# A fused attention and mixer kernel on one core: half of the second row's probabilities turned by DMA, its values in two float16 parts

## The chip, the core and the metric

The kernel runs on one core of one Trainium2 chip. The metric is device time in microseconds (us) of one execution. The engines are TensorE (PE, with its weight loads as PEld), VectorE (DVE), ScalarE (ACT), GpSimd (POOL) and SyncE (SP, which here issues nearly all DMA transfers).

## The reference

Two batch rows of 768 positions go through three stages. q and k are scaled random normals, v is 0.1 times a random normal; n_global is 8 and n_local 96, so each query tile of 128 positions sees its own tile, the one before it, and a few global columns.

```python
scores = scale * q @ k.T - slope[h] * dist        # 8 heads of 64; masked where not keep
a = exp(scores - max); a = a / (sum(a) + 1e-9)
x = (a @ v)                                        # 2 x 768 x 512
x = x + relu(layernorm(x) * g @ w_ch1) @ w_ch2     # 512 -> 2048 -> 512
u = x + (relu(x.T @ w_tok1) @ w_tok2).T            # over the 768 positions, 256 wide
out = u + relu(u @ w_ch1') @ w_ch2'                # 512 -> 1536 -> 512
```

## The kernel before

The work is cut into 12 row tiles T of 128 positions: T = 0 to 5 are the first batch row, T = 6 to 11 (`SPLIT` = 6 and up) the second. All float32 products of the MLPs are made of three float16 products: each factor is split into a high and a low part, and `mm3` (L372 to L374) adds high x high, high x low and low x high in PSUM.

Attention of one tile is `window_tile` (L400). It handles the 8 heads in four pairs p. For each two pairs PE makes the scores (L453, a PSUM tile `S`); DVE adds bias and takes the row minimum (L469, tile `ex`); ACT takes the exponential (L474); PE turns the probabilities, 128x128 at a time, by float32 transposes against an identity (L479, PSUM tile `T`). From there the rows differ:

- First row: ACT or DVE copies the turned probabilities to `pt` (L515, L518), and PE multiplies by V in float32 (L484).
- Second row: ACT writes their float16 high part `ph`, scaled by 2^15 (L501), DVE the rest `pl` (L503), and `pv3` multiplies on PE by V, which is held in three bfloat16 parts `vb` with a column of ones: three matmuls per head and key block, of 130, 64 and 130 columns (L497 to L499). The three parts of V cost two casts and two subtractions per tile (L423 to L430: one cast on DVE, one on ACT, both subtractions on GpSimd). A pair has four transposes and 12 such matmuls; in tile 6, which has one key block only, half of that.

In all 24 pairs of the second row there are 88 transposes and 88 groups of three matmuls.

Then come layer norm (`norm_ops`), a float16 split of the normed tile and its transposition by a DMA on SP (`turn_ops`, L580, tiles `xh` to `xa` or `xb`), and the first MLP in passes over groups of three tiles. Attention is spread between the MLP's matmuls. Weights come as doubles: SP loads 512 KB to `stg` (L166), ACT and DVE repack them (L744 `fw`, L750 `wf`) and split them (L766, L772 or L769 on GpSimd); the split weights are stored to DRAM (L725) and loaded again for later passes (L715).

The order of every engine's instructions is made ahead of time by a planner (`Plan`). Each operation has an engine, an estimated cost and a due time `prio`; the constants `AHEAD`, `SLOT`, `DUE`, `EARLY`, `LEAD`, `HEAD` and others set the due times, and strings such as `LOB1` or `FE` say which engine takes which operation. While PE would have nothing to do in the first stretch, the planner puts in filler matmuls (L106). Each engine then runs its own queue strictly in this order; SP's queue too, so a transfer that waits holds back the ones behind it.

`Guard` collects sums of squares of inputs and intermediate tiles (ACT, L671) and checks at the end that all lie in ranges in which the float16 splits are exact enough; if not, a slow general path runs again.

Of the kernel before, what the change touches and what calls it, by code (L numbers as in the profile page):

```python
# [12 lines left out]
F16 = mybir.dt.float16  # L13
# [17 lines left out]
PSC = 2.0 ** 15  # L31
# [361 lines left out]
def copy_on(nc, eng, out, src):  # L393
    if eng == "A":
        nc.scalar.activation(out=out, in_=src, func=AF.Copy)
    else:
        nc.vector.tensor_copy(out, src)


def window_tile(o, plan, prio, T, slot):  # L400
# [41 lines left out]
    for p in range(4):  # L442
# [89 lines left out]
        if p == 3 and 0 < t < NT - 1:  # L532
# [100 lines left out]
class Guard:  # L633
# [4 lines left out]
          "z": (86, 90, 0.0, 60000.0), "g": (90, 91, 0.125, 16.0)}  # L638
    N = 91
# [430 lines left out]
AHEAD = {'s': -8.81, 'k': 53.46, 'q': -8.16, 'v': 42.47}  # L1070
STORE, RELOAD = 53.17, 7.48

LOA1 = 'GVGGVVVVVGGVVGVV'
LOB1 = 'GGGGVGVGVGVVGVVV'
LOA2 = 'GGGVVVVVVGVG'
LOB2 = 'VVVVVVGVVVGV'
LOT = 'VGG'
NLO, ULO = 'GGVGGGGGVVGV', 'VGVVVGVGGVVG'
TURN = 2.5
UP = 19.85  # L1080
MK0, MK1, MK2 = 'VVVVAAAA', 'VAVVAAAA', 'AVVVAVAA'
# [19 lines left out]
WIDE = {'hid': 5, 'wa': 5, 'wb': 5, 'stg': 3, 'fw': 2, 'wf': 2, 'st': 2, 'xn': 1, 'mn': 3, 'sum': 3, 'ex': 3, 'pt': 2, 'ph': 2, 'pl': 2, 'ao': 2, 'xz': 3, 'sx': 8, 'raw0': 1, 'raw1': 1, 'xa': 1, 'xb': 1, 'm': 2, 'k': 2, 's': 2, 't': 2}  # L1101
SIZES = {**WIDE, 'hid': 12, 'wa': 8, 'wb': 8, 'wf': 4, 'fw': 3, 'stg': 4, 'xn': 2, 'xh': 2, 'uh': 2, 'xz': 3, 'sz': 4}

# [178 lines left out]
class WindowAttention:  # L1282
    def __init__(self, o):
# [5 lines left out]
        o.vb = ap.tile([P, 3, H, 3, D + 1], BF16, name="vb")  # L1289

    def ops(self, o, plan, prio):
# [3 lines left out]
        plan.op("G", 0.3, 20.0, lambda: nc.gpsimd.memset(o.vb[:, :, :, 0, D:], 1.0), w=[("vb", z, 0) for z in range(3)])  # L1295
        plan.op("G", 0.5, 20.0, lambda: nc.gpsimd.memset(o.vb[:, :, :, 1:, D:], 0.0), w=[("vb", z, i) for z in range(3) for i in (1, 2)])
# [179 lines left out]
```

## Time and profile before

| what | us |
|---|---|
| median of 3 runs | 553.74 (553.57 to 555.43) |
| the profiled execution | 554.65 |
| its span, first to last instruction | 552.9 |
| PE busy | 543.2 |
| DVE busy | 408.9 |
| ACT busy | 334.9 |
| POOL busy | 178.0 |

The mean granted clock of PE is 0.993 of full speed. The span is read from the profile's page; the 1.75 us between it and the execution's time lie around it. A matmul's duration in the trace covers its way through the array, and consecutive matmuls overlap; what a matmul costs the queue is the distance from its start to the next one's start. In the same way ACT and DVE instructions overlap their neighbours by some 0.1 us, so their cost is read as start to start.

### The profile page before, as it was taken

The numbers are of one execution on the slowest core, as the hardware profiler recorded it, in microseconds if no ns is written. First come the engines' busy times: TensorE is split into PE (matmuls) and PEld (weight loads), VectorE is DVE, ScalarE is ACT, GpSimd is POOL, SyncE is SP. The second block draws the span as 40 slices with busy tenths as digits, with TensorE's granted clock in tenths as the row PEclk, the third lists the DMA queues.
The fourth block names the chain that finished last, engine by engine and source line by source line (L and its number), as shares of the span: only waits on it lengthen the run. The fifth ranks groups of instructions, "written<-read, shape, count | busy, mean of one in ns | idle before, by whom it ended". The sixth has DMA issues, their size and how long they took to land.

```text
span 552.9 us, 9384 instructions
## 1 busy us (share of the span) xinstructions
PE 543.2 (98%) x3267; PEld 310.7 (56%) x3267; DVE 408.9 (74%) x909; ACT 334.9 (61%) x747; POOL 178.0 (32%) x185
## 2 busy tenths in 40 slices
PE   8999999999999999999999999999999999999995
PEld 6777766746656555554555555455445545555542
DVE  7778889977599554579888986899987777654431
ACT  6778778966848334745877655667785554534210
POOL 2233574660411023363322236502151563110000
PEclk9999999999999999999999999999999999999998
DMA  8877997796869757312674460047564342302012
GB/s 252 217 194 230 236 279 238 202 287 203 272 238 282 258 106 185 111 58 61 187 178 157 162 152 21 1 153 223 201 181 123 107 157 77 115 1 76 2 39 82
DMA packets 87596, 87.09 MB, mean 158 GB/s; under 512 B 46836, under 2 KB 61172, under 8 KB 87540
## 3 DMA queue, kind: packets, MB, share of 16 engines
q1 hardware_dynamic: 87538, 86.40, 53.6%
q8 instruction: 28, 0.46, 0.4%
q14 instruction: 28, 0.23, 0.1%
q10 hardware_dynamic: 2, 0.00, 0.0%
HBM read 61.87 MB, written 17.83 MB: 144 GB/s over the span
## 4 chain that ended last, share of the span: by engine, by line
PE 94%; DVE 2%; ACT 2%; issue 1%; POOL 0%; POOLq 0%; ACTq 0%
PE L L372 12%; PE L L374 12%; PE L L373 12%; PE L2S L374 9%; PE L2S L373 9%; PE L2S L372 9%; PE chain L372 4%; PE chain L374 4%; PE chain L373 4%; PE S L453 4%; PE T L479 3%; PE PV L484 2%; PE tok L374 2%; PE tok L372 2%; PE tok L373 2%
## 5 line engine op out<-in xcount | busy, mean ns | idle before, releaser
L372 PE MATMUL L2S<-wb,h 128*128 128x512 f16 x228 | 86.4, 379 | 0.0
L373 PE MATMUL L2S<-wb,h 128*128 128x512 f16 x228 | 86.4, 379 | 0.0
L374 PE MATMUL L2S<-wb,h 128*128 128x512 f16 x228 | 86.4, 379 | 0.0
L889 DVE SCALAR_TENSOR_TENSOR x<-L2S,x 128x512 f32<-128x512 f32 x57 | 39.2, 688 | 49.7 <-PE L2S L374 49.7
L374 PEld LDWEIGHTS <-h 128*128 128x128 f16 x336 | 32.9, 98 | 39.6
L744 ACT ACTIVATE fw<-stg 128x512 f16<-128x512 bf16 x62 | 48.0, 776 | 10.5 <-DMA stg<-in_moe_w_ch_dram 7.2
L372 PEld LDWEIGHTS <-h 128*128 128x128 f16 x336 | 32.8, 98 | 36.8 <-issue 0.7
L373 PEld LDWEIGHTS <-h 128*128 128x128 f16 x336 | 32.9, 98 | 35.8
L474 ACT ACTIVATE ex<-ex,mn 128x256 f32<-128x256 f32 (+1 forms) x96 | 41.6, 480 | 14.1 <-DVE mn L469 13.9
L823 POOL TENSOR_TENSOR sz<-Q,sz 128x512 f16<-128x512 f32 x18 | 22.4, 1242 | 84.6 <-ACT sz L915 84.6
L750 DVE SCALAR_TENSOR_TENSOR wf<-stg,fw 128x512 uint32<-128x512 uint32 x62 | 44.8, 736 | 0.4 <-DMA scr_1b<-wb 0.4
L372 PE MATMUL L<-wb,h 128*128 128x512 f16 x108 | 41.0, 379 | 0.0
L374 PE MATMUL L<-wb,h 128*128 128x512 f16 x108 | 40.9, 379 | 0.0
L373 PE MATMUL L<-wb,h 128*128 128x512 f16 x108 | 40.9, 379 | 0.0
L364 DVE SCALAR_TENSOR_TENSOR h<-L,h 128x384 f16<-128x384 f32 x40 | 22.2, 555 | 22.5 <-ACT h L358 22.2
L823 POOL TENSOR_TENSOR Q<-wa 128x512 f32<-128x512 f16 x18 | 25.9, 1438 | 38.8 <-DVE wa L772 18.5
L372 PEld LDWEIGHTS <-wa 128*128 128x128 f16 x268 | 26.2, 98 | 19.6 <-issue 2.7
L374 PEld LDWEIGHTS <-wa 128*128 128x128 f16 x268 | 26.2, 98 | 17.3
L373 PEld LDWEIGHTS <-wa 128*128 128x128 f16 x268 | 26.2, 98 | 17.0
L889 DVE SCALAR_TENSOR_TENSOR x<-L,x 128x512 f32<-128x512 f32 x27 | 18.6, 690 | 22.2 <-PE L L374 22.1
L372 PE MATMUL L<-xa,wa 128*128 128x384 f16 x104 | 34.0, 326 | 0.0
L373 PE MATMUL L<-xa,wa 128*128 128x384 f16 x104 | 33.9, 326 | 0.0
(233 smaller groups left out, 1417.7 us busy)
## 6 DMA issues: line engine op xcount, KB each, us to landing
stg<-in_moe_w_ch_dram SPq DMA_DIRECT2D x56, 512.0 KB, 4.6
wa<-scr_1a SPq DMA_DIRECT2D x24, 256.0 KB, 3.7
wb<-scr_1b SPq DMA_DIRECT2D x24, 256.0 KB, 4.0
scr_1a<-wa SPq DMA_DIRECT2D x16, 256.0 KB, 6.8
scr_1b<-wb SPq DMA_DIRECT2D x16, 256.0 KB, 3.5
K<-in_k_dram SPq DMA_DIRECT2D x12, 256.0 KB, 3.9
Q<-in_q_dram SPq DMA_DIRECT2D x12, 256.0 KB, 4.4
V<-in_v_dram SPq DMA_DIRECT2D x12, 256.0 KB, 4.0
```

What stands on the lines that cost most here:

```text
L364: nc.vector.scalar_tensor_tensor(out=lo(), in0=src(), scalar=0.0, in1=plain(hi()), op0=ALU.max, op1=ALU.subtract)
L372: nc.tensor.matmul(ps, ah, bh, start=first, stop=False, **k)
L373: nc.tensor.matmul(ps, ah, bl, start=False, stop=False, **k)
L374: nc.tensor.matmul(ps, al, bh, start=False, stop=last, **k)
L453: nc.tensor.matmul(bs[j].t[:, i, :w], o.Q[r, qs, p + i, :], o.K[r, slots, p + i, :], start=True, stop=True)
L474: nc.scalar.activation(out=ex.t[:, j, :w], in_=ex.t[:, j, :w], func=AF.Exp, bias=mn.t[:, h:h + 1], scale=-1.0)
L479: nc.tensor.transpose(bt.t[:, j, i, :], ex.t[:, j, i * P:(i + 1) * P], o.ident[:])
L484: nc.tensor.matmul(bv.t[:, 2 * (p % 2) + j], pt.t[:, j, i, :], o.V[:, z, 2 * p + j], start=(i == 0), stop=(i == n - 1))
L744: op("A", 0.66, prio - 2, lambda: nc.scalar.activation(out=fw.t[:, :, 1], in_=stg.t[:, 4:2049:4].bitcast(BF16), func=AF.Copy, scale=2.0 if ...
L750: op("V", 0.6, prio - 1, lambda: nc.vector.scalar_tensor_tensor(out=raw().bitcast(U32), in0=stg.t.bitcast(U32)[:, 1:1024:2], scalar=13, in ...
L823: op(eng, {"G": 0.1 + n * 0.00227, "V": 0.07 + n * 0.00104}[eng], prio, lambda: e.tensor_tensor(out=out(), in0=a(), in1=b(), op=alu), lock ...
L889: n = op("V", 0.6, prio, lambda: nc.vector.scalar_tensor_tensor(out=x[:], in0=b.t[:], scalar=BACK if o.half else 1.0, in1=x[:], op0=ALU.mu ...
```

## The change

1. V of the second row is held in two float16 parts, scaled by 2^8, not three bfloat16 parts. Per tile ACT writes the high part (`AF.Copy` with scale), DVE the low part (`scalar_tensor_tensor`), and ACT a sum of squares of V for the range check (kind "v", six more columns). GpSimd's two subtractions and one cast go away.
2. `pv3` issues two matmuls per head and key block, of 130 columns (high probabilities x both parts of V) and of 65 (low probabilities x high part of V), not three.
3. A string `PT` marks each of the 24 pairs of the second row P or D; 12 are D: two of tile 6, two of tile 8, one of tile 9, four of tile 10, three of tile 11. For a D pair ("turned") ACT and DVE split the unturned probabilities `ex` into a tile `pq` of 8 blocks, and one DMA transpose on SP's queue turns all of them into `ph`. The PE transposes and their PSUM tile go away for it. The D pairs of tile 6 have 4 blocks, the ten others 8. So 10 x 4 + 2 x 2 = 44 PE transposes are gone.
4. The planner's constants and engine strings are set anew, which orders everything anew.

```diff
-        op("G", 1.15, pvr, lambda: nc.gpsimd.tensor_tensor(out=v, in0=v, in1=V[:, :, 0, :D], op=ALU.subtract),
-           r=[("vb", c, 0)], w=[("v", c)])
...
-        op("G", 1.15, pvr, lambda: nc.gpsimd.tensor_tensor(out=V[:, :, 2, :D], in0=v, in1=V[:, :, 1, :D], op=ALU.subtract),
-           r=[("v", c), ("vb", c, 1)], w=[("vb", c, 2)])
+        op("A", 0.54, pvr, lambda: nc.scalar.activation(out=V[:, :, 0, :D], in_=v, func=AF.Copy, scale=VSC), r=[("v", c)],
+           w=[("vb", c, 0)])
+        op("V", 0.6, pvr, lambda: nc.vector.scalar_tensor_tensor(
+            out=V[:, :, 1, :D], in0=v, scalar=VSC, in1=V[:, :, 0, :D], op0=ALU.mult, op1=ALU.subtract),
+           r=[("v", c), ("vb", c, 0)], w=[("vb", c, 1)], lock=True)
+        o.guard.square("v", pvr + GUARDX, lambda: v, [("v", c)])
...
-                        nc.tensor.matmul(bv.t[:, j], ph.t[:, j, i, :], o.vb[:, z, h, 0:2], start=(i == 0), stop=False)
-                        nc.tensor.matmul(bv.t[:, j, 1, :D], ph.t[:, j, i, :], o.vb[:, z, h, 2, :D], start=False, stop=False)
-                        nc.tensor.matmul(bv.t[:, j], pl.t[:, j, i, :], o.vb[:, z, h, 0:2], start=False, stop=(i == n - 1))
...
+                        a = j * n + i
+                        nc.tensor.matmul(bv.t[:, j], pt.t[:, a], o.vb[:, z, h], start=(i == 0), stop=False)
+                        nc.tensor.matmul(bv.t[:, j, 0], pt.t[:, 2 * n + a], o.vb[:, z, h, 0], start=False, stop=(i == n - 1))
...
+            op("A", 0.06 + 0.23 * n if turned else 0.05 + 0.215 * n, prio(k + slot["T"]), lambda part=part, src=src: nc.scalar.activation(
+                out=part(0), in_=src(), func=AF.Copy, scale=PSC), r=keys, w=dst[:1], get=[pq] if turned else [])
+            op("V", 0.3 * n, prio(k + slot["T"]), lambda part=part, src=src: nc.vector.scalar_tensor_tensor(
+                out=part(1), in0=src(), scalar=PSC, in1=part(0), op0=ALU.mult, op1=ALU.subtract),
+               r=[*keys, dst[0]], w=dst[1:], lock=turned)
+            if turned:
+                op("S", TURN * n / 2, prio(k + slot["T"]), lambda pt=pt, pq=pq: nc.sync.dma_start(
+                    pt.t[:, :4 * n], pq.t[:, :4 * w], transpose=True), r=dst, w=[(pt, 0), (pt, 1)], get=[pt])
...
-AHEAD = {'s': -8.81, 'k': 53.46, 'q': -8.16, 'v': 42.47}
+AHEAD = {'s': 29.29, 'k': 79.79, 'q': -33.06, 'v': -59.46}
...
+PT = 'PDPDPPPPDPDPPPPDDDDDDDDP'
...
-HEAD = 85.06
-DUE = [36.2, 20.0, 77.7, 9.05]
+HEAD = 56.45
+DUE = [32.72, 16.66, 78.81, 48.03]
```

What this moves is shown at three places.

**TensorE, attention of tile 10, before.** An MLP matmul, then the transposes of two pairs (`T`), then the next MLP matmuls; 24 rows further on the first group of three value matmuls (`PV`).

```order
L374 LDWEIGHTS wa_1968
L374 MATMUL L1_2462<-xb_897,wa_1968 128x384
L479 MATMUL T_2488<-ident_127,ex_2450 128x128 x4
L479 MATMUL T_2495<-ident_127,ex_2454 128x128 x4
L372 LDWEIGHTS wa_1976
```

```order
L497 LDWEIGHTS ph_2489
L497 MATMUL PV_2530<-vb_232,ph_2489 128x130
L498 LDWEIGHTS ph_2489
L498 MATMUL PV_2530<-vb_232,ph_2489 128x64
L499 LDWEIGHTS pl_2490
L499 MATMUL PV_2530<-vb_232,pl_2490 128x130
```

**The same stretch of TensorE after** (a turned pair of tile 10).

```order
L373 MATMUL L1_2294<-xb_914,wa_1909 128x384
L374 LDWEIGHTS wa_1909
L374 MATMUL L1_2294<-xb_914,wa_1909 128x384
L498 LDWEIGHTS ph_2256
L498 MATMUL PV_2323<-vb_232,ph_2256 128x130
L499 LDWEIGHTS ph_2256
L499 MATMUL PV_2323<-vb_232,ph_2256 128x65
```

The transposes of a turned pair are gone from this queue, and a group is two matmuls; the 65-column one reads the blocks of the low part from the same tile `ph`.

**SP's queue in the same stretch, before**: weight loads (`stg`), stores and reloads of split weights (`scr`, `wb`), a load of global K columns and a copy inside `vb`.

```order
L535 DMA K_58<-in_k_dram 128x4x32
L160 DMA K_58<-in_k_dram 128x512
L715 DMA wb_2059<-scr_1b4_1978 128x1024
L715 DMA wb_2064<-scr_1b5_2002 128x1024
L715 DMA wb_2099<-scr_1b6_2015 128x1024
L725 DMA scr_1b7_2116<-wb_1571 128x1024
L166 DMA stg_61<-in_moe_w_ch1_dram 128x4x512
L539 DMA vb_232<-vb_232 32x1560
L166 DMA stg_61<-in_moe_w_ch1_dram 128x4x512
L715 DMA wb_2175<-scr_1b7_2116 128x1024
L166 DMA stg_61<-in_moe_w_ch1_dram 128x4x512
L166 DMA stg0_203<-in_moe_w_ch1_dram 128x4x512
```

**After:**

```order
L515 DMA_TRANSPOSE ph_2033<-pq_1990 128x8x128
L166 DMA stg_61<-in_moe_w_ch2_dram 128x2048 x2
L515 DMA_TRANSPOSE ph_2110<-pq_2066 128x8x128
L550 DMA vb_232<-vb_232 32x1040
L546 DMA K_58<-in_k_dram 128x4x32
L515 DMA_TRANSPOSE ph_2144<-pq_2083 128x8x128
L166 DMA stg_61<-in_moe_w_ch2_dram 128x2048
L515 DMA_TRANSPOSE ph_2188<-pq_2148 128x8x128
L166 DMA stg0_203<-in_moe_w_ch2_dram 128x2048
L166 DMA stg_61<-in_moe_w_ch1_dram 128x4x512
L515 DMA_TRANSPOSE ph_2256<-pq_2190 128x8x128
L166 DMA stg_61<-in_moe_w_ch1_dram 128x4x512
```

The DMA transposes of turned pairs stand between the weight loads; each waits for DVE's second part of `pq`, and the `stg` loads behind it are issued after it. The reloads of this pass stand ahead of the stretch.

**ScalarE in the head, before**: from the first exponentials of tile 3 to the split of the normed tile 2 (`xh`). `fw` and `wa` or `wb` are weights being repacked and split.

```order
L474 ACTIVATE ex_612<-ex_612,mn_613 128x256 x2
L744 ACTIVATE fw1_63<-stg_61 128x512
L474 ACTIVATE ex_628<-ex_628,mn_613 128x256
L515 ACTIVATE pt_634<-T_633 128x512
L474 ACTIVATE ex_628<-ex_628,mn_613 128x256
L744 ACTIVATE fw2_204<-stg_61 128x512
L766 ACTIVATE wa_667<-wf_651 128x512
L515 ACTIVATE pt_661<-T_660 128x512
L613 ACTIVATE xn_679<-x2_66,st_654 128x512
L474 ACTIVATE ex_669<-ex_669,mn_613 128x256 x2
L474 ACTIVATE ex_674<-ex_674,mn_613 128x256 x2
L576 ACTIVATE xh_700<-xn_679 128x512
```

**After**, up to the norm of tile 2 (`xn`):

```order
L755 ACTIVATE fw2_204<-stg_61 128x512
L777 ACTIVATE wa_638<-wf_619 128x512
L526 ACTIVATE pt_624<-T_623 128x512
L473 ACTIVATE ex_630<-ex_630,mn_631 128x256 x2
L473 ACTIVATE ex_642<-ex_642,mn_631 128x256 x2
L755 ACTIVATE fw0_62<-stg_61 128x512
L526 ACTIVATE pt_658<-T_657 128x512
L777 ACTIVATE wa_686<-wf_655 128x512
L526 ACTIVATE pt_681<-T_680 128x512
L777 ACTIVATE wb_694<-wf_677 128x512
L755 ACTIVATE fw1_63<-stg0_203 128x512
L624 ACTIVATE xn_711<-x2_66,st_689 128x512
```

More weight work stands between the exponentials: until the 40th exponential (the end of tile 4) ScalarE's queue now holds 11 `fw` where it held 6, 8 splits of weights where it held 4, and 16 copies `pt` where it held 14.

## Rows read from the trace of the kernel before

**Rows 1.** The page's part 1: busy us, share of the span, instructions of each engine.

```profile
PE 543.2 (98%) x3267; PEld 310.7 (56%) x3267; DVE 408.9 (74%) x909; ACT 334.9 (61%) x747; POOL 178.0 (32%) x185
```

**Rows 2.** Windows: stretch, length, PE, PEld, DVE, ACT, POOL busy; PEclk, DMA share, GB/s.

```profile
0.00:20.00 20.00, 18.04 (x122) 13.46 (x122) 15.66 (x74) 14.28 (x40) 4.28 (x32) 1.00 0.89 254
20.00:40.00 20.00, 19.40 (x155) 16.11 (x155) 15.42 (x61) 14.41 (x31) 7.16 (x11) 1.00 0.69 180
40.00:58.00 18.00, 17.08 (x117) 13.19 (x116) 13.31 (x47) 16.48 (x35) 5.71 (x7) 0.91 0.78 232
58.00:80.00 22.00, 22.00 (x173) 15.65 (x172) 18.15 (x60) 15.60 (x36) 14.47 (x13) 1.00 1.00 259
80.00:110.00 30.00, 30.00 (x257) 20.62 (x254) 27.56 (x72) 27.54 (x64) 16.94 (x15) 1.00 0.77 225
110.00:150.00 40.00, 40.00 (x276) 23.34 (x274) 26.94 (x64) 28.56 (x67) 14.70 (x14) 1.00 0.80 249
150.00:200.00 50.00, 50.00 (x355) 29.98 (x354) 38.03 (x92) 28.02 (x54) 5.86 (x6) 1.00 0.72 236
200.00:552.00 352.00, 346.70 (x1830) 178.31 (x1828) 253.80 (x445) 190.02 (x428) 108.90 (x92) 1.00 0.40 114
```

**Rows 3.** Waits of PE: line, what it waited for, us in total, times, longest.

```profile
PE T L479 <- ACT ex L474: 0.8, 2, 0.4
PE PV L484 <- ACT pt L515: 0.6, 1, 0.6
```

**Rows 4.** Chain that ended last, three pieces: start us, us, what.

```profile
31.37 1.06 PE S L453 x8
...
40.58 2.01 PE S L453 x8
...
152.07 0.44 PE T L479 x4
```

**Rows 5.** Timeline of PE at two pairs of the second row: start, duration, instruction.

```profile
196.62 0.33 PE L374 MATMUL L<-xa,wa 128*128 128x384 f16 x1
196.79 0.22 PE L497 MATMUL PV<-vb,ph 128*128 128x130 bf16 x1
196.84 0.20 PE L498 MATMUL PV<-vb,ph 128*128 128x64 bf16 x1
196.88 0.22 PE L499 MATMUL PV<-vb,pl 128*128 128x130 bf16 x1
196.93 0.22 PE L497 MATMUL PV<-vb,ph 128*128 128x130 bf16 x1
...
197.96 0.33 PE L372 MATMUL L<-xb,wa 128*128 128x384 f16 x1
```

**Rows 6.** Line L580, the DMA transposes: issue time ns and landing us, min/median/max.

```profile
L580 SPq DMA_TRANSPOSE xb<-xh x9: 1232/1238/1289, 54.4 to 428.4; - x9
...
DMA to landing us min/median/max: 3.0/3.2/6.2
```

**Rows 7.** Groups of ACT and of DVE: count, busy us, mean ns, idle before.

```profile
L501 ACT ACTIVATE ph<-T 128x512 f16<-128x512 f32 (+1 forms) x24 | 12.5, 559 | 6.3 <-PE T L479 6.2
L671 ACT ACTIVATE junk<-x 128x512 bf16<-128x512 f32 x24 | 14.9, 622 | 16.0 <-DVE x L889 15.2 <-DVE x L1057 0.6
L503 DVE SCALAR_TENSOR_TENSOR pl<-T,ph 128x512 f16<-128x512 f32 (+1 forms) x24 | 14.6, 640 | 1.4 <-ACT ph L501 1.3
```

**Rows 8.** Timeline of ACT in the head: start, duration, instruction.

```profile
45.14 0.62 ACT L766 ACTIVATE wa<-wf 128x512 f16<-128x512 f32 x1
45.66 0.89 ACT L474 ACTIVATE ex<-ex,mn 128x256 f32<-128x256 f32 x2
46.46 0.77 ACT L744 ACTIVATE fw<-stg 128x512 f16<-128x512 bf16 x1
47.10 0.56 ACT L515 ACTIVATE pt<-T 128x512 f32<-128x512 f32 x1
47.56 0.50 ACT L474 ACTIVATE ex<-ex,mn 128x256 f32<-128x256 f32 x1
```

More of the change, by code (lines that the diff above doesn't have):

```diff
@@ L460, in window_tile @@
         pt = Buf("pt", lambda: o.sm.tile([P, 2, 2, P], F32, tag="pt", name="pt", bufs=2))
-        bt = psum_buf(o, "T", [2, 2, P])
+        turned = T >= SPLIT and PT[4 * (T - SPLIT) + p] == "D"
+        bt = None if turned else psum_buf(o, "T", [2, 2, P])
         if T >= SPLIT:
-            pt = Buf("ph", lambda: o.sm.tile([P, 2, 2, P], F16, tag="ph", name="ph", bufs=2))
-            pl = Buf("pl", lambda: o.sm.tile([P, 2, 2, P], F16, tag="pl", name="pl", bufs=2))
+            pt = Buf("ph", lambda: o.sm.tile([P, 8, P], F16, tag="ph", name="ph", bufs=o.sizes["ph"]))
+            pq = Buf("pq", lambda: o.sm.tile([P, 8 * P], F16, tag="pq", name="pq", bufs=o.sizes["pq"]))
             bv = psum_buf(o, "PV", [2, 2, D + 1])
@@ L490, in window_tile, with pv3 @@
             op("A", 0.3 if n == 1 else 0.4, prio(k + slot["exp"]), lambda j=j, expo=expo: expo(j), r=[(mn, p, j)], w=[(ex, j)])
-        op("T", 0.22 * n, prio(k + slot["T"]), probs, r=[(ex, 0), (ex, 1)], w=[(bt, 0)], get=[bt, pt] + ([pl] if T >= SPLIT else []))
+        if not turned:
+            op("T", 0.22 * n, prio(k + slot["T"]), probs, r=[(ex, 0), (ex, 1)], w=[(bt, 0)], get=[bt, pt])
         if T >= SPLIT:
-            def pv3(p=p, ph=pt, pl=pl, bv=bv):
+            def pv3(p=p, pt=pt, bv=bv):
                 for j in range(2):
@@ new lines, in pv3 @@
+                        nc.tensor.matmul(bv.t[:, j, 0], pt.t[:, 2 * n + a], o.vb[:, z, h, 0], start=False, stop=(i == n - 1))
+            if turned:
+                part = lambda i, y=pq: y.t[:, i * 2 * w:(i + 1) * 2 * w].rearrange("p (j c) -> p j c", j=2)
+                src = lambda ex=ex: ex.t[:, :, :w]
+                keys, dst = [(ex, 0), (ex, 1)], [(pq, 0), (pq, 1)]
+            else:
+                part = lambda i, y=pt: y.t[:, i * 2 * n:(i + 1) * 2 * n].rearrange("p (j i) c -> p j i c", j=2)
+                src = lambda bt=bt: bt.t[:, :, :n]
+                keys, dst = [(bt, 0)], [(pt, 0), (pt, 1)]
@@ L507, in window_tile @@
+            if turned:
+                op("S", TURN * n / 2, prio(k + slot["T"]), lambda pt=pt, pq=pq: nc.sync.dma_start(
+                    pt.t[:, :4 * n], pq.t[:, :4 * w], transpose=True), r=dst, w=[(pt, 0), (pt, 1)], get=[pt])
+            op("T", 0.18 * n, prio(k + slot["PV"]), pv3, r=[(pt, 0), (pt, 1), *vkeys], w=[(bv, 0)], get=[bv])
             if PVE[T - SPLIT] == "A":
@@ L539, in window_tile @@
                 op("S", 0.3, prio(k + slot["gk"]), lambda: nc.sync.dma_start(o.vb[:NGF, c], o.vb[:NGF, prev]),
-                   r=[("vb", prev, i) for i in range(3)], w=[("vb", c, i) for i in range(3)])
+                   r=[("vb", prev, i) for i in range(2)], w=[("vb", c, i) for i in range(2)])
     if T >= SPLIT:
         def inverse():
-            nc.vector.tensor_scalar(out=sm.t[:], in0=ao.t[:, :, 0, D], scalar1=1e-9 * PSC, scalar2=None, op0=ALU.add)
+            nc.vector.tensor_scalar(out=sm.t[:], in0=ao.t[:, :, 0, D], scalar1=1e-9 * PSC * VSC, scalar2=None, op0=ALU.add)
             nc.vector.reciprocal(out=sm.t[:], in_=sm.t[:])
@@ L1065, in token_ops @@
         transpose_ops(o, plan, prio(14 + 2 * i), "uT", lambda T=T: o.x[T][:], [*xk(T), ("tk",), *r], dst, key, get)
-AHEAD = {'s': -8.81, 'k': 53.46, 'q': -8.16, 'v': 42.47}
[L1071 to L1081, printed above, removed]
+AHEAD = {'s': 29.29, 'k': 79.79, 'q': -33.06, 'v': -59.46}
+STORE, RELOAD = 42.03, 10.48
+LOA1 = 'VGGVVGGVGVGGVVGG'
+LOB1 = 'GGVGVVGGGVVGGGGV'
+LOA2 = 'VGVVVGVVVGGG'
+LOB2 = 'VVGVGGVGVVGG'
+LOT = 'GGG'
+NLO, ULO = 'VGVVVVVVVGGG', 'GGGGVGVGGGVV'
+TURN = 2.2
+PT = 'PDPDPPPPDPDPPPPDDDDDDDDP'
+UP = -65.03
+MK0, MK1, MK2 = 'VVVVAAAA', 'AAVAAAAV', 'AAVAVVAV'
 HEAD0 = -200.0
-MASK2 = -121.51
+MASK2 = -122.88
 BUSY = 10, 3
-HOLD = [-39.73, 27.18, 27.27]
+HOLD = [-99.44, -5.02, 7.93]
 FIRST = [("k", 0), ("q", 0), ("k", 1), ("q", 1), ("v", 0), (1, "a", 0), ("v", 1), (1, "a", 1), ("k", 2), ("q", 2), (1, "a", 2), ("v", 2)]
@@ L1100 @@
 PSUMS = ('m', 's', 't', 'k')
[L1101 to L1102 removed]
+WIDE = {'hid': 5, 'wa': 5, 'wb': 5, 'stg': 3, 'fw': 2, 'wf': 2, 'st': 2, 'xn': 1, 'mn': 3, 'sum': 3, 'ex': 3, 'pt': 2, 'ph': 2, 'pq': 2, 'ao': 2, 'xz': 3, 'sx': 8, 'raw0': 1, 'raw1': 1, 'xa': 1, 'xb': 1, 'm': 2, 'k': 2, 's': 2, 't': 2}
+SIZES = {**WIDE, 'hid': 12, 'wa': 8, 'wb': 8, 'wf': 4, 'fw': 3, 'stg': 4, 'xn': 2, 'ph': 3, 'pq': 2, 'xh': 2, 'uh': 2, 'xz': 3, 'sz': 4}
 def store(o, T):
@@ L1288, in __init__ @@
         o.bmh = ap.tile([P, H, 3, P], BF16, name="bmh")
-        o.vb = ap.tile([P, 3, H, 3, D + 1], BF16, name="vb")
+        o.vb = ap.tile([P, 3, H, 2, D + 1], F16, name="vb")
     def ops(self, o, plan, prio):
```

44 lines of the change are left out of this document (17 added, 27 removed).

## The prediction

> **What bounds the kernel now.** I read the busy times first, then PE by stretch, then PE's waits, the chain of work that ended last, and at last the places that the edit touches. PE is busy for 543.2 of 552.9 us [rows 1]. By stretch [rows 2] it has no gap at all from 58 to 200 us, where attention of the second row runs between the MLP's matmuls, and what it lacks after 200 us is the tail behind its last matmul. Before 58 us it is short of work: 2.0, 0.6 and 0.9 us of gaps in three windows, filler matmuls in others, and in the third a mean granted clock of 0.91, mostly in one place where eight score matmuls took 2.01 us, not the 1.06 of the same eight elsewhere [rows 4]. The waits that the profile names for PE are short, 0.8 and 0.6 us, and both are for ScalarE in attention [rows 3]. So from 58 us on an instruction taken from PE's queue shortens the kernel by what it occupied there, as long as the other queues keep up. Before 58 us the chain through attention and ScalarE decides, and there taking work from PE gives nothing.
>
> **The change part by part.** *Transposes.* 44 float32 transposes leave PE. Four stand in the chain with 0.44 us [rows 4], so 0.11 us each: 44 x 0.11 = 4.8 us. All belong to the second row, in the stretch without gaps, so the whole of it counts.
>
> *Value matmuls.* Two pairs, 24 matmuls in 8 groups, ran from 196.79 to 197.96 us [rows 5]: 1.17 us, 0.146 per group. Within a group the 130-column matmul holds the queue 0.05 us, the 64-column one 0.04, the last 0.05. A new group is one of 130 and one of 65 columns: 0.05 to 0.055 plus 0.037, which gives 0.092 and saves 0.054. Were each matmul to take the mean of 1.17 / 24 = 0.049 us whatever its columns, it would save 0.049; were time proportional to columns (195 of 324), 0.058. Over 88 groups: 4.8 us, between 4.3 and 5.1. I take the middle, since the rows show time following columns with a small floor.
>
> Here a rule stands against the row. The Trainium skill, TensorE: Matmul & The Clock Gate, section Back-to-back issue gap, gives about 81 ns for each pair of weight load and matmul at 128 columns in a real kernel, more than columns alone would ask. By that, fewer columns would give nothing and a matmul less 0.081 us, 7.1 us over 88. The row's 0.049 us disagrees.
>
> *ScalarE and VectorE, second row.* Splitting unturned probabilities costs ACT and DVE what splitting turned ones costs now, 24 instructions of 0.56 us and 24 of 0.64 [rows 7], only from SBUF. V's parts: ACT keeps one 512-element pass per tile and gets a sum of squares (0.62 us each, six in all [rows 7]); DVE changes a cast for a two-operand pass, below 0.64 us each; GpSimd loses 12 subtractions. That is under 8 us on queues that are 56 to 92% busy between 58 and 200 us [rows 2]. Cost at the end: nothing, because PE's 142 us of queued work hides it; without that cover it would be up to 8 us.
>
> *DMA transposes.* 12 new ones, as large as those of the normed tiles (ten) or half (two). Each of these occupies SP 1.24 us and lands 3.2 us after issue, 6.2 at most [rows 6]. Queued behind the wait for `pq` are the `stg` loads shown in the order above, and for those ACT and DVE wait. A turned pair's way from scores to value matmuls is then: two minima 0.7, two exponentials 0.8, the split 0.5 and 0.6, issue 1.2 and landing 3.2, about 7 us. PE's order puts between the scores and the value matmuls of the tightest turned pair of 8 blocks (tile 9) 48 MLP matmuls of 384 columns at 0.165 [rows 5], eight scores at 0.26 (two passes each), four transposes and four groups: about 10.8 us. So some 3.8 us are left for queueing. I take nothing, and the wait that is late next is ACT's in the head. DMA is busy 72 to 100% there [rows 2]; the transposes add 12 x at most 3.2 us if nothing overlaps, in 142 us: up to 27%, which fits from 110 us on (72 to 80% busy) and not between 58 and 80 us.
>
> *The new order in the head.* Up to the 40th exponential ACT has 5 `fw`, 4 splits and 2 copies more, which start to start take 0.64, 0.52 and 0.46 us [rows 8]: 3.2 + 2.1 + 0.9 = 6.2 us of weight work put ahead of attention. In the 58 us of the head ACT was idle for 5.7 + 5.6 + 1.5 = 12.8 us [rows 2], nearly all of it waits for attention itself. If the weights are in when ACT is idle, the 6.2 us disappear in these gaps; if not, attention and with it PE shifts by up to 6.2 us, which nothing later gives back. The other way, the slow clock and PE's waits could go: 0.09 x 18 = 1.6 us of clock; I bound the gain at 1.5. I take a loss of 1.5 us, nearer to the gain since the gaps are twice the extra work, and keep -1.5 and +6.2.
>
> *Sum.* 552.9 - 4.8 - 4.8 + 1.5 = 544.8 us of span. The profiled execution had 1.75 us around its span, so 546.55; it was 0.91 us above the median of the runs, so **545.6 us**. The bounds together: 552.9 - 4.8 - 5.1 - 1.5 = 541.5, as a median 542.3, and 552.9 - 4.8 - 4.3 + 6.2 = 550.0, as a median 550.8.
>
> **The rivals.** *A: the head takes the gain back.* Besides ACT's work, five weight loads of 0.5 MB are issued earlier: 2.5 MB at 255 GB/s [rows 2] is 10 us of DMA in a head where DMA had 11 to 31% free, some 12 us. If loads of keys and queries fall behind these, ACT's 6.2 us and 3 us of late tiles add up: 552.9 - 9.6 + 9 = 552.3, as a median 553.1, no change. For it: the head is bound by attention, and the chain there is one of latencies. Against it: ACT and DVE have gaps, and weights are then ready for the stretch after.
>
> *B: turned pairs hold PE up, slower than before.* SP's queue is in order, and DVE serves `pq` in order. If on average a turned pair's way grows from 7 past 10.8 us, PE stands, with nothing else queued. From 1.0 us of standing per turned pair on (12 us, against 9.6 - 1.5 = 8.1 gained and 2.8 of measurement) the kernel is slower; at 2 us per pair it is 552.9 - 8.1 + 24 = 568.8, as a median 569.6, as no later stretch has room. For it: landing takes up to 6.2 us [rows 6], and DMA is full from 58 to 80 us. Against it: most turned pairs come after 110 us, where DMA is 72 to 80% busy, and the others have up to 7 us more cover than the tightest.
>
> The Trainium skill, VectorE: DVE Perf Modes, section Rules for kernel authors, takes this side: turn 128x128 on TensorE if PSUM is a possible destination, by DMA otherwise. It counts single latencies (390 against 1309 ns); the rows have 0.11 us of queue against a transfer off the queue.
>
> *C: small matmuls at a fixed price*, the 81 ns above as a mechanism: a weight load before each small matmul sets the pace. With 0.049 us per matmul it is in the lower bound of the saving already; at a pace that gives 7.1 us for the groups, 552.9 - 4.8 - 7.1 + 1.5 = 542.5, as a median 543.3.
>
> *D: the range check fails* and the general path runs too. V is about 0.1 times normal, so 512 squares sum to some 5, between the bounds 2^-7 and 2^15. I give it nothing.
>
> **How the numbers follow.** Forecast 0.80 (542.3 to 550.8), A 0.11 (551 to 554), B 0.06, C 0.03. About 0.5%, 2.8 us, is what a measurement of this kernel can tell from no change: faster is below 551.0, slower above 556.5. Faster: 0.80 + 0.03 and 0.02 of A = 0.85; same 0.09; slower 0.06. The range of 8 in 10 is 542 to 551.5: the forecast's bounds and the near end of A.
>
> **What would show it.** Right: T matmuls fall from 176 to 132, PV groups of two start 0.09 us apart, PE has no gap between 62 and 540 us, and first MLP matmuls start at 48 to 52 us. Step by step wrong: PE waiting for DMA `ph` (B); PE waiting for ACT `ex` or `pt` in the head by more than 6 us in all (A); a group that takes 0.1 us or more (the value matmuls' term). Most at risk is the term of the head, as no row shows ACT's new order.

## The result and the profile after

The changed kernel took 546.38 us (median of four runs, 544.98 to 548.01) beside 554.37 us for the kernel before; the ratio is 0.9856, with a 95% interval of 0.9821 to 0.9891. Five more runs later gave 546.99 us and a ratio of 0.9866 (0.9846 to 0.9886). So it is 1.3 to 1.4% faster, and the forecast of 545.6 us (542.0 to 551.5) was 0.8 to 1.4 us too low. The profiled execution took 546.87 us with a span of 545.1; the one before had 552.9. An execution more than 1.5% above the fastest of its kernel counts as slow and is left out of medians and ratios; there was one, in the run with more turned pairs.

The rows of after answer those of before in the same order. The page's part 1, for [rows 1]:

```profile
PE 532.0 (98%) x3132; PEld 299.7 (55%) x3132; DVE 408.6 (75%) x902; ACT 337.1 (62%) x760; POOL 163.2 (30%) x181
```

PE lost 11.2 us of busy time, ACT and DVE hardly changed, and GpSimd lost 14.8 us, nearly all of them its subtractions. By stretch, for [rows 2] (length; PE, PEld, DVE, ACT, POOL busy; clock, DMA share, GB/s):

```profile
0.00:20.00 20.00, 17.02 (x121) 12.86 (x122) 14.74 (x71) 14.79 (x42) 4.07 (x33) 1.00 0.86 251
20.00:40.00 20.00, 17.70 (x142) 14.45 (x141) 17.52 (x64) 18.42 (x39) 5.70 (x9) 1.00 0.91 239
40.00:58.00 18.00, 16.67 (x115) 12.75 (x115) 14.12 (x41) 13.19 (x27) 6.94 (x8) 0.91 0.91 248
58.00:80.00 22.00, 22.00 (x151) 14.95 (x150) 21.25 (x57) 17.11 (x38) 4.42 (x4) 1.00 0.84 252
80.00:110.00 30.00, 29.89 (x219) 18.36 (x218) 23.95 (x80) 23.16 (x62) 5.78 (x6) 1.00 0.70 192
110.00:150.00 40.00, 40.00 (x286) 24.11 (x284) 31.07 (x84) 32.74 (x78) 10.38 (x9) 1.00 0.85 212
150.00:200.00 50.00, 50.00 (x319) 27.39 (x317) 37.32 (x81) 27.18 (x53) 16.07 (x13) 1.00 0.82 223
200.00:545.00 345.00, 338.73 (x1793) 174.80 (x1790) 248.64 (x431) 190.48 (x428) 109.80 (x99) 1.00 0.43 129
```

From 58 to 200 us PE has one gap of 0.11 us: the turned pairs did not hold it up. Before 58 us its gaps grew from 3.5 us to 3.0 + 2.3 + 1.3 = 6.6 us, ACT is busy for 18.42 of the 20 us from 20 to 40 (14.41 before), and DMA for 91% of the time from 20 to 58 us, where it was 69 and 78%. PE's waits, for [rows 3]:

```profile
PE PV L483 <- ACT pt L526: 3.2, 3, 1.6
PE T L478 <- ACT ex L473: 1.0, 2, 0.6
PE PV L483 <- DMA V<-in_v_dram: 0.7, 2, 0.5
```

All are in the first row's attention, in the head; none names `ph`. A turned pair of the second row, for [rows 5]: four groups from 150.71 to 151.06 us are 0.088 us each, of which the 130-column matmul holds the queue for 0.06 us and the 65-column one for 0.03.

```profile
150.71 0.22 PE L498 MATMUL PV<-vb,ph 128*128 128x130 f16 x1
150.77 0.19 PE L499 MATMUL PV<-vb,ph 128*128 128x65 f16 x1
150.80 0.22 PE L498 MATMUL PV<-vb,ph 128*128 128x130 f16 x1
...
151.06 0.38 PE L372 MATMUL L<-wb,h 128*128 128x512 f16 x1
```

The 12 new DMA transposes, for [rows 6] (issue time in ns and landing in us, min/median/max), cost what the old ones did:

```profile
L515 SPq DMA_TRANSPOSE ph<-pq x12: 1190/1260/1785, 84.4 to 169.0; - x12
...
DMA to landing us min/median/max: 2.5/3.3/5.7
```

### The profile page after: what moved, and what is told of

Same layout as the page of the kernel before. It is cut to its first block, busy times and chain, and to the rows that moved or that the text cites. A ratio compares the mean times of both kernels' runs of the same rounds, so it can differ in the third digit from the quotient of the medians.

```text
span 545.1 us, 9103 instructions
## 1 busy us (share of the span) xinstructions
PE 532.0 (98%) x3132; PEld 299.7 (55%) x3132; DVE 408.6 (75%) x902; ACT 337.1 (62%) x760; POOL 163.2 (30%) x181
## 4 chain that ended last, share of the span: by engine, by line
PE 84%; ACT 6%; DVE 4%; DMA 2%; SPq 1%; issue 1%; POOL 0%; ACTq 0%
PE L L372 11%; PE L L374 11%; PE L L373 11%; PE L2S L372 9%; PE L2S L374 9%; PE L2S L373 9%; PE chain L372 4%; PE chain L374 4%; PE chain L373 4%; PE S L451 3%; DMA stg<-in_moe_w_ch_dram 2%; PE tok L373 2%; PE tok L372 2%; PE tok L374 2%; ACT ex L473 2%; PE T L478 2%
## 5 line engine op out<-in xcount | busy, mean ns | idle before, releaser
L834 POOL TENSOR_TENSOR Q<-Q 128x256 f32<-128x256 f32 x36 | 31.5, 874 | 32.6 <-DVE Q L834 31.2
L372 PE MATMUL L<-xa,wa 128*128 128x384 f16 x104 | 34.0, 327 | 0.0
L373 PE MATMUL L<-xa,wa 128*128 128x384 f16 x104 | 33.9, 326 | 0.0
L374 PE MATMUL L<-xa,wa 128*128 128x384 f16 x104 | 33.9, 326 | 0.0
```

Source lines behind the costliest of these rows:

```text
L372: nc.tensor.matmul(ps, ah, bh, start=first, stop=False, **k)
L373: nc.tensor.matmul(ps, ah, bl, start=False, stop=False, **k)
L374: nc.tensor.matmul(ps, al, bh, start=False, stop=last, **k)
L834: op(eng, {"G": 0.1 + n * 0.00227, "V": 0.07 + n * 0.00104}[eng], prio, lambda: e.tensor_tensor(out=out(), in0=a(), in1=b(), op=alu), lock ...
```

## The experiments

All differences below are taken against the changed kernel's second measurement, 546.99 us, unless another is named. The intervals of two ratios together make a difference of two kernels uncertain by some 1.4 us, and by 2.1 us where the run with the old constants and all transposes on PE is one of the two.

**The changed kernel again.** No edit.

> The changed kernel once more, beside the three below, for a narrower interval. Both theories: 545 to 547.5 us, a ratio to the kernel before of 0.983 to 0.988.

Measured: 546.99 us, as expected. Its profiled execution had a span of 547.6 us where the other had 545.1. The order of the instructions is the same; the difference stands in the head, at the clock:

```profile
40.00:58.00 18.00, 17.30 (x100) 13.86 (x100) 12.28 (x38) 12.95 (x26) 5.69 (x7) 0.72 0.76 218
```

The mean granted clock of this stretch was 0.72, not 0.91. In both executions PE stood for 1.2 to 1.5 us before 38.7 us, and between 41 and 42 us the clock went to its lower level (0.50); in the one it was back at full by 46 us, in the other by 52, and the first MLP matmul started at 53.08 and at 55.00 us. So 2 us of a measurement of this kernel go with how long the low clock lasts in the head. All nine executions of it fit: the five with a mean granted clock of 0.996 or 0.997 took 544.98 to 546.87 us, the four with 0.986 to 0.990 took 546.99 to 549.44 us.

**Value matmuls put back to three**, order of the queues as it is.

```diff
-  nc.tensor.matmul(bv.t[:, j, 0], pt.t[:, 2 * n + a], o.vb[:, z, h, 0], start=False, stop=(i == n - 1))
+  nc.tensor.matmul(bv.t[:, j, 1, :D], pt.t[:, 2 * n + a], o.vb[:, z, h, 1, :D], start=False, stop=False)
+  nc.tensor.matmul(bv.t[:, j], pt.t[:, 2 * n + a], o.vb[:, z, h], start=False, stop=(i == n - 1))
```

> The changed kernel with three value matmuls per group (130, 64 and 130 columns, as before the change) and every queue's order else as it is; the extra one adds a product of the two low parts, which changes the result by less than its rounding. If a value matmul is paid by its place in TensorE's queue (0.146 against 0.092 us per group), 88 groups cost 4.8 us (4.3 to 5.1) more than the changed kernel: 551.2 us. If the gain of the groups was hidden behind other waits, less than 2 us more. If each matmul cost a fixed 0.08 us, 7.1 us more: 553.5.

Measured: 551.77 us, 4.8 us more by the medians, 4.2 by the ratios (0.9941, 0.9924 to 0.9958). The value matmuls are worth their place in PE's queue; a fixed price per matmul, 7.1 us, lies outside.

**Transposes put back on PE**, DMA transposes left in.

```diff
-            bv = psum_buf(o, "PV", [2, 2, D + 1])
+            bv = Buf("t", lambda: bank(o, "PV", 4, 2 * D))
...
+                for _ in range(2 * n if turned else 0):
+                    nc.tensor.transpose(bv.whole[:, 3], o.ident[:], o.ident[:])
```

> The changed kernel with 44 float32 transposes of 128x128 put back on TensorE ahead of the value matmuls of the turned pairs (they turn the identity into an unused part of the PSUM bank; the DMA transposes stay). Order of the queues else as it is. If a transpose is paid by its place in the queue, 44 x 0.11 = 4.8 us more than the changed kernel: 551.2 us. If turned pairs in fact made TensorE wait for the DMA, the transposes would fall into that wait and cost less than 2 us.

Measured: 551.29 us, 4.3 us more by medians and by ratios (0.9943, 0.9924 to 0.9962). The 44 transposes too are worth about their place in the queue (0.11 us each makes 4.8), and did not fall into waits.

**The old constants, all transposes on PE.** Of the change V's two parts are left, and with them a third buffer of `ph` and a few estimated costs in the planner.

```diff
-PT = 'PDPDPPPPDPDPPPPDDDDDDDDP'
+PT = 'PPPPPPPPPPPPPPPPPPPPPPPP'
...
-AHEAD = {'s': 29.29, 'k': 79.79, 'q': -33.06, 'v': -59.46}
+AHEAD = {'s': -8.81, 'k': 53.46, 'q': -8.16, 'v': 42.47}
...
-HEAD = 56.45
+HEAD = 85.06
-LEAD = -178.69
+LEAD = -208.54
```

> Only the edit of V (two float16 parts, two matmuls per group, the sum of squares) under the constants of the kernel before; all transposes on TensorE. If the value matmuls are worth their place in TensorE's queue and the head is as before: 554.6 - 4.8 = 549.8 us (ratio 0.991). If part of that is hidden: 551 to 554.

Measured: 549.65 us beside 554.54 for the kernel before (ratio 0.9902, 0.9870 to 0.9933): 4.9 us gained, where 4.8 were forecast for the value matmuls; the interval leaves 3.7 to 7.2 us. Of ACT's and DVE's extra work for V, the six sums of squares among it, nothing is seen at the end. And it measures the head: with the old order PE's first MLP matmul started at 47.33 us, and the clock did not fall:

```profile
40.00:58.00 18.00, 17.29 (x128) 13.15 (x130) 15.09 (x49) 16.91 (x36) 4.90 (x7) 1.00 0.94 261
```

The kernel with the transposes put back has the same PE work as this one and the new order, and takes 551.29 - 549.65 = 1.6 us more. The other way, 549.65 - 4.8 = 544.85 us would be the changed kernel without a loss; it has 546.99, so 2.1 us. That is the price of the new order, 1.6 to 2.1 us by medians and uncertain by about as much. It differs between executions, and with the clock: one with the transposes put back took 549.48 us, within this run's 549.32 to 550.17 (clock 0.997 or 0.998), and another 553.16 us at a mean clock of 0.989.

**The old constants with the turned pairs.** As the last one, but `PT` as in the change.

> Both edits (two float16 parts of V, 12 turned pairs) under the planner constants and engine strings of the kernel before, so that the head is ordered as before, without the extra weight work on ScalarE. If the edits are worth 9.2 to 9.6 us and the new order in the head costs 2 to 3 us: 554.6 - 9.4 = 545.2 us or a little less, 1 to 2.5 us below the changed kernel. If the new order of the head costs nothing (the constants fit the edits): 547 us or above, with waits of TensorE for ph or pt after 58 us.

Measured: 566.22 us (ratio 1.0202, 1.0167 to 1.0236), 11.7 us slower than the kernel before and 21 us above the 545.2 expected. Both expectations are missed by far, and it is rival B: 21 us over 12 turned pairs is 1.75 us per pair. Not all of it is standing: from 58 to 200 us PE's gaps sum to 14.8 us, 1.2 us per pair, and most of the rest is the low clock that comes with them. The loss lies where the turned pairs are (columns as in [rows 2]):

```profile
110.00:150.00 40.00, 30.58 (x225) 18.23 (x222) 31.34 (x90) 26.86 (x60) 13.93 (x13) 0.86 0.84 197
150.00:200.00 50.00, 45.79 (x254) 24.16 (x253) 31.99 (x56) 28.52 (x55) 4.70 (x4) 0.98 0.84 278
```

PE stands for 9.4 and 4.2 us in these two stretches, and its clock falls with it, to 0.86 over the first 40 us. Its longest waits:

```profile
PE PV L498 <- DMA ph<-pq: 4.5, 2, 3.8
...
PE L L372 <- ACT junk L682: 2.5, 1, 2.5
PE PV L498 <- DMA vb<-vb: 2.2, 1, 2.2
```

SyncE's timeline at three of the transposes, and the PE row that waited for the second of them:

```profile
131.82 1.27 SPq L515 DMA_TRANSPOSE ph<-pq  x1
135.50 1.24 SPq L515 DMA_TRANSPOSE ph<-pq  x1
138.76 2.33 SPq L515 DMA_TRANSPOSE ph<-pq  x1
...
142.15 0.29 PE L498 MATMUL PV<-vb,ph 128*128 128x130 f16 x1 [3.83 <-DMA ph<-pq]
...
142.31 0.30 PE L498 MATMUL PV<-vb,ph 128*128 128x130 f16 x1
```

Three transposes follow each other after 3.7 and 3.3 us, and the second one's value matmuls start 6.6 us after its issue, which is a late landing and not a late issue. Only a part of the standing time bears the name of `ph`, though; other waits (`vb`, ACT, DVE) come in the same stretch.

**All pairs on PE**, under the new constants.

```diff
-PT = 'PDPDPPPPDPDPPPPDDDDDDDDP'
+PT = 'PPPPPPPPPPPPPPPPPPPPPPPP'
```

> The changed kernel with all 24 pairs of the second row marked P: the 12 DMA transposes and their tile pq go, 44 transposes return to TensorE, the rest of the change stays, and the planner orders anew. If the 44 transposes are worth their place in TensorE's queue and the DMA's way is hidden: 4.3 to 4.8 us above the changed kernel's 547.0, so 551.3 to 551.8 us. If the turned pairs hold TensorE up or cost something on ScalarE, VectorE or DMA: less, 547 to 550.

Measured: 553.27 us, 6.3 us more (ratio 0.9970, 0.9951 to 0.9990). 4.3 to 4.8 of these are the transposes; the other 1.5 to 2 us can be the new plan or the clock of its head (0.72 from 40 to 58 us in the profiled execution). The run does not tell these apart.

**All pairs by DMA.**

```diff
-PT = 'PDPDPPPPDPDPPPPDDDDDDDDP'
+PT = 'DDDDDDDDDDDDDDDDDDDDDDDD'
```

> The changed kernel with all 24 pairs marked D: 44 further transposes leave TensorE, 12 more DMA transposes join SyncE's queue. If the way of a turned pair stays hidden everywhere: 4.3 to 4.8 us below the changed kernel's 547.0, so 542.2 to 542.7 us. If the tightest pairs (four turned pairs per tile one after the other, two pq tiles, DMA full from 58 to 80 us) run out of cover, TensorE waits for the DMA's ph: from 0.4 us per new pair on nothing is gained (547), at 1 us per pair it is 554.

Measured: 567.78 us (ratio 1.0239, 1.0204 to 1.0275), 21 us more than the changed kernel, and rival B again. The stretch (columns as in [rows 2]):

```profile
110.00:150.00 40.00, 27.02 (x188) 16.11 (x188) 31.19 (x80) 25.32 (x60) 12.78 (x12) 0.83 0.84 194
```

PE's waits:

```profile
PE S L451 <- DVE mn L468: 6.9, 3, 2.9
...
PE L L372 <- DMA wa<-scr_1a: 3.3, 2, 1.9
PE PV L498 <- DMA ph<-pq: 2.6, 4, 1.2
PE PV L498 <- DMA vb<-vb: 1.6, 1, 1.6
```

PE stands for 13 us between 110 and 150. `ph` itself is named for 2.6 us only: the rest is late minima on DVE, late weights and a late copy in `vb`, of which the last two are issued by SyncE, in the queue that holds the transposes. From 58 to 200 us PE stands for 14.8 us, as under the old constants, and the low clock (0.83 and 0.93 in the last two stretches to 200 us) adds to it.

**More turned pairs** (tiles 6 and 7, with the head of the run on loads below).

```diff
-PT = 'PDPDPPPPDPDPPPPDDDDDDDDP'
+PT = 'DDDDDDDDDPDPPPPDDDDDDDDP'
```

> The last run's head (weight work moved behind attention's) with six more turned pairs, all of tiles 6 and 7, which come between 80 and 112 us, where 24 turned pairs left TensorE without a gap. 20 more transposes leave TensorE. If those pairs have cover: 20 x 0.11 = 2.2 us and the head's 1 to 2 us below the changed kernel's 547.0, so 543 to 544 us. If their DMA transposes push the transfers of the following tiles back, gaps come after 112 us and it is 547 us or above.

Measured: 559.71 us (ratio 1.0087, 1.0062 to 1.0112). No gap from 58 to 110 us, where the new pairs are, and 5.9 us of gaps from 110 to 150 us at a clock of 0.93: the second expectation by its time and place. That the new pairs' transposes push later transfers back is not shown: `ph` is named for 1.4 us only, DVE and ACT for more, and the planner ordered everything anew here too. The head of this execution had a clock of 0.72 from 40 to 58 us besides.

**Each transpose issued twice.**

```diff
-                op("S", TURN * n / 2, prio(k + slot["T"]), lambda pt=pt, pq=pq: nc.sync.dma_start(
-                    pt.t[:, :4 * n], pq.t[:, :4 * w], transpose=True), r=dst, w=[(pt, 0), (pt, 1)], get=[pt])
+                op("S", TURN * n / 2, prio(k + slot["T"]), lambda pt=pt, pq=pq: [nc.sync.dma_start(
+                    pt.t[:, :4 * n], pq.t[:, :4 * w], transpose=True) for _ in range(2)], r=dst, w=[(pt, 0), (pt, 1)], get=[pt])
```

> The changed kernel with each of the 12 DMA transposes of turned pairs issued twice, the second after the first has landed; order of the queues else as it is. A turned pair's way grows by some 3.3 + 1.2 = 4.5 us, and SyncE's queue stands as long. If the cover is as forecast (way 7 us, tightest pair 10.8 us, others up to 7 us more), only the tightest pairs run out: 547 to 550 us. If the changed kernel's order leaves no more room than its transposes need, every pair stalls by about 4 us: 570 us or more. If SyncE's queue counts beyond the pair itself, TensorE waits for weights (wa, wb) or for vb, not for ph.

Measured: 580.97 us, 34 us more, 2.8 us per pair. Two rows of SyncE's timeline:

```profile
164.12 6.20 SPq L515 DMA_TRANSPOSE ph<-pq  x2
...
171.54 8.74 SPq L515 DMA_TRANSPOSE ph<-pq  x2
```

PE's waits:

```profile
PE PV L498 <- DMA ph<-pq: 12.9, 6, 4.3
PE PV L498 <- DMA vb<-vb: 6.1, 2, 3.2
```

The stretch with most of the loss (columns as in [rows 2]):

```profile
150.00:200.00 50.00, 35.00 (x198) 17.42 (x197) 24.71 (x63) 20.80 (x45) 10.13 (x9) 0.86 0.75 164
```

The twelve double issues take 3.7 to 8.7 us, 5.7 in the mean and so 4.4 more than one. The expectation by my cover (547 to 550) falls, but not by the pairs alone. PE stands for 23.6 us from 58 to 210 us, 2.0 us per pair; most of the other 10 us is the low clock. And `ph` is named for 12.9 us of the standing. That is about what the room of each pair in the changed kernel's own trace (1.7 to 5.6 us, read in the next section) would let through: 4.4 us less that room, summed over the twelve pairs, makes some 13 us, an estimate. The third expectation holds as well: the copy in `vb`, which SyncE issues in the same queue, is named for 6.1 us.

**Three moves in the head.** In the changed kernel the scores of tile 4 start at 42.90 us, in the kernel before at 40.51. The timeline of ACT, then of PE, then of SyncE, on the way to them in the changed kernel:

```profile
37.35 0.77 ACT L755 ACTIVATE fw<-stg 128x512 f16<-128x512 bf16 x1 [1.58 <-DMA stg<-in_moe_w_ch_dram]
37.99 0.57 ACT L526 ACTIVATE pt<-T 128x512 f32<-128x512 f32 x1
...
38.61 0.44 PE L483 MATMUL PV<-V,pt 128*128 128x65 f32 x2 [1.18 <-ACT pt L526]
39.53 1.78 PE L483 MATMUL PV<-V,pt 128*128 128x65 f32 x14 [0.48 <-DMA V<-in_v_dram]
41.85 1.12 PE L478 MATMUL T<-ident,ex 128*128 128x128 f32 x4 [0.55 <-ACT ex L473]
...
35.37 0.61 SPq L548 DMA_DIRECT2D V<-in_v_dram  x1
36.08 1.29 SPq L591 DMA_TRANSPOSE xa<-xh  x1
37.45 0.58 SPq L546 DMA_DIRECT2D K<-in_k_dram  x1
38.09 0.61 SPq L160 DMA_DIRECT2D K<-in_k_dram  x1
```

A weight repacking (`fw`) waits for its load, and the copy that PE needs stands behind it. I took these limits away one after the other, by moving operations back in the finished plan, with all that depends on them. `LATER` names the operations by number: (a, b) puts a behind b. (The first run's edit picks its two operations by their place in ScalarE's queue instead.)

```diff
+        for n, m in LATER if self.WARM != (0, 0) else ():
+            a, b = self.seq.index(self.ops[n]), self.seq.index(self.ops[m])
+            moved, rest = [self.ops[n]], []
+            for y in self.seq[a + 1:b + 1]:
+                (moved if y.deps & {z.n for z in moved} else rest).append(y)
+            self.seq[a:b + 1] = rest + moved
```

First the two repackings behind the copies (630 and 681 are `fw` operations):

> The changed kernel with two weight repackings of ScalarE moved behind the copies of turned probabilities that they held up in the head: the first one behind one instruction, the seventh (which waited 1.58 us for its load, and TensorE behind it 1.18 us) behind three. Nothing else moves but what depends on them. If the loss in the head (2 to 3 us) comes from ScalarE waiting in order for a weight's load, 1.2 to 2.4 us less than the changed kernel: 544 to 545.2 us. If the head is bound by DMA itself (the load of V that comes next, the keys), under 0.6 us less.

Measured: 546.91 us, no gain. PE reached the value matmuls 2 us earlier and waited there for V (rows of PE):

```profile
36.42 0.33 PE L493 MATMUL PV<-V,pt 128*128 128x65 f32 x2
38.73 2.99 PE L493 MATMUL PV<-V,pt 128*128 128x65 f32 x14 [1.98 <-DMA V<-in_v_dram]
```

Then, with these, a weight load and a store on SyncE behind V's rows: `LATER = [(630,44), (681,163), (643,557), (686,557), (687,177)]`.

> As the run that moved two weight repackings behind the copies, and now on SyncE too: one weight load (512 KB) and one store of split weights (256 KB) go behind the load of V's global rows and the DMA transpose that follow them in the head, and the repacking that reads this load goes behind the next four exponentials. If V's global rows came late because weight traffic ran beside them (TensorE waited 1.98 us for V at 38.7 us), that wait falls below 0.7 us and the kernel gains 1 to 2 us on the changed kernel's 547.0: 545 to 546 us. If the rows come late for another reason (they are issued only when the last value matmuls of the tile before are done), the wait stays above 1.3 us and the time at 546.5 to 547.

Measured: 548.86 us (ratio 0.9903, 0.9889 to 0.9918), 1.9 us more. V's wait is gone, as the first theory said, and nothing is gained:

```profile
36.33 2.24 PE L489 MATMUL PV<-V,pt 128*128 128x65 f32 x16
...
42.29 1.23 PE L457 MATMUL S<-K,Q 64*128 64x256 f32 x4 [1.97 <-issue]
```

The profile names no releaser for the last wait; the scores read K, whose loads are issued at 37.6 and 38.2 us. So, third, K's loads ahead of the DMA transpose: (557, 221) added.

> As the run that moved loads later, and the DMA transpose of the normed tile 1 goes behind the two loads of K that follow it on SyncE. In the kernel before, the scores of tile 4 began at 40.51 us; in the changed kernel at 42.90, with ScalarE's wait removed at 42.51, with V's wait removed too at 42.29, each time when K, issued at 37.5 to 38.2 us behind the DMA transpose, has just landed. If SyncE's late issue of K is what sets the head, these scores begin at 40.4 to 41 us, TensorE's wait before them falls from 1.97 to below 0.5 us, and the time is 1.5 to 2.5 us below that run's 548.9 and some 0.5 us around the changed kernel's 547.0 or below. If something else sets it, the scores stay at 42 us or later and the time at 547 to 549.

Measured: 549.26 us (ratio 0.9908, 0.9895 to 0.9922). The scores start at 40.54 us, as in the kernel before, and the wait before them is gone: it was K's late issue that set their start. The time does not follow (timeline of PE, then of ACT):

```profile
40.54 1.13 PE L457 MATMUL S<-K,Q 64*128 64x256 f32 x8
...
44.73 1.11 PE L489 MATMUL PV<-V,pt 128*128 128x65 f32 x8 [2.46 <-ACT pt L532]
...
43.46 0.77 ACT L761 ACTIVATE fw<-stg 128x512 f16<-128x512 bf16 x1 [2.54 <-DMA stg<-in_moe_w_ch_dram]
```

The weight load that was moved is late now, `fw` waits 2.54 us for it, and a copy stands behind `fw` again. In all of these kernels first MLP matmuls start at 53.0 to 55.3 us. Weight loads, V and K share a DMA that is 91% busy from 20 to 58 us in the changed kernel's first profile, and in each of the three runs the transfer that was put later, or the next one, is what PE ends up waiting for. None of the versions beats the changed kernel. The low clock comes in all three profiles too (0.84, 0.81 and 0.81 from 40 to 58 us), so their times do not measure the waits alone.

## Why the prediction was right, and where not

*Transposes, 4.8 us.* Right within the measurement: 4.3 us when put back alone. T matmuls fell from 176 to 132.

*Value matmuls, 4.8 us.* Right: 4.8 when put back alone, 4.9 when they are the only edit. The pitch of a group is 0.088 us where 0.092 was forecast. The Trainium skill, TensorE: Matmul & The Clock Gate, section Back-to-back issue gap, gives about 81 ns per pair of weight load and matmul at 128 columns, so 0.16 us for the two of a group, an estimate from its figure; the trace has 0.088, at full clock. The 4.2 to 4.8 us that came back with the third matmul have no room for rival C.

*ACT, DVE and the sums of squares, 0 us.* Right within 1.7 us: 4.9 of 4.8 us arrived with them in.

*The head, 1.5 us (-1.5 to 6.2).* Near: 1.6 to 2.1 us, but uncertain by about 2, so that the size proves little. Of the mechanism, ACT standing in order behind a weight, and PE behind ACT, is in the trace: 4.2 us of PE's waits are for `pt` and `ex`, under the 6 us that would have been rival A. That the loads of the extra weight work are the root, and make V and K late as well, is argued and not shown: three runs that moved such work or such loads gained nothing. The clock was counted as a possible gain only; in the changed kernel it is part of the loss, as the executions with the lower mean clock are the slower ones. The first MLP matmul at 48 to 52 us was wrong (53.08), and partly meant nothing, as the new order puts one more round of attention ahead of it.

*DMA transposes, 0 us.* Right in size, with a wrong reason. The tightest turned pair of 8 blocks was said to be tile 9's, with 3.8 us left, others with up to 7 us more. In the changed kernel its transpose is issued at 137.93 us and its value matmuls start at 145.17, 7.2 us later; with 3.3 us of landing 3.9 are left. So that pair was read well. But a pair of tile 8 has less:

```profile
107.58 0.62 SPq L550 DMA_DIRECT2D vb<-vb  x1
108.24 1.30 SPq L515 DMA_TRANSPOSE ph<-pq  x1
...
113.23 0.22 PE L498 MATMUL PV<-vb,ph 128*128 128x130 f16 x1
```

Here 5.0 us lie between, so 1.7 are left; of the twelve pairs three have 5.0 to 5.1 us and the others 6.6 to 8.9. My step counted what stands in PE's queue from the scores on, and let the way begin at once; DVE and ACT take a pair later than that, and SyncE's queue can hold it too, so the way from the scores is longer than 7 us and the rest of the cover smaller. For the pair of tile 8, which was not looked at for itself, DVE's part of `pq` is done at 106.07 us, and the transpose is issued 2.2 us later, behind a copy in `vb`. The two runs with other orders and the one with doubled transposes show how thin it was: 21, 21 and 34 us. Rival B did not happen in this order, but under the old constants it came to 566.2 us, near its price of 569.6 at 2 us of standing per pair; the way there was another, 1.2 us of standing per pair and the low clock.

*The sum.* 545.6 us was 0.8 to 1.4 us low. The head's 0.1 to 0.6 us more and the transposes' 0.5 us less are of that size, but the executions of the changed kernel differ by more, 544.98 to 549.44 us. Of the signs, no gap of PE between 62 and 540 us came nearly true: 1.4 us, 1.3 of them after 500 us.

The Trainium skill, VectorE: DVE Perf Modes, section Rules for kernel authors, prefers TensorE for 128x128 where PSUM can take the result. The runs agree with it under the old constants, where 12 turned pairs cost 16.6 us (549.65 against 566.22), and disagree under the new ones, where taking the 44 transposes off TensorE saves 4.3.

What stays open: how much of the head's price is the low clock and how much the waits before it, which of the constants makes the head's loads come early, and whether an order exists that has the old head with the new tail. It was not found by moving single operations.

## What to carry to other kernels

Work taken off a saturated engine's queue is worth its start-to-start distance, and two edits add up, as long as what replaces it has cover; read the cover of every pair and not of one, and double the replacement to see what else hangs on its queue. The order that goes with such an edit is part of the edit: the same twelve turned pairs gained under one set of constants and lost 16.6 us against all pairs on TensorE under the other. Where several loads are late by about the same amount, as in this head, removing the wait that the profile names only shows the next one.

## What the runs showed of the hardware

- What the granted clock does after a short stall of TensorE differs between executions of one kernel, and the length of the wait does not tell it. In the changed kernel, after 1.2 and 1.5 us of standing before 38.7 us, it was at the lower level for some 3.4 us in one execution and 10 us in another, and the spans differ by 2.5 us. In the kernel before it was there for 3.4 us from 41 us on, behind a longest wait of 0.4 us in that stretch. Under the old constants with all transposes on PE, with waits of 0.6 us, it did not fall at all. Two microseconds of the kernel before:

```profile
42.00:44.00 2.00, 2.00 (x12) 1.49 (x9) 2.00 (x8) 1.45 (x4) 0.00 (x0) 0.53 0.55 159
```

- A DMA transpose of 8 blocks takes SyncE 1.2 to 1.3 us, mostly, and lands after 3.3 us (2.5 to 5.7 in the changed kernel). Issued twice, the second waiting for the first, the two take 4.4 to 8.7 us of SyncE's queue, and 3.7 us for a pair of four blocks.
- At the lower clock (0.50 from 142 to 143 us under the old constants) a group of two value matmuls takes 0.16 us (142.15 to 142.31 us), at the full one 0.088: 1.8 times as long at half the clock, so most of a group's time follows TensorE's clock.
